# First-pair loads, the mask row table and an early second chunk in the opening of a block-sparse attention and gated FFN kernel

## The chip, the cores and the metric

The kernel runs on one core of a Trainium2 chip. The metric is device time in microseconds (us): 293.34 as the median of four runs. All times below are those of one profiled execution unless another source is named; its clock starts at the first instruction of the program.

## The reference

```python
scores = (q @ k.transpose(0, 1, 3, 2)) / np.sqrt(64)     # q, k, v: 4 x 8 heads x 768 x 64
mask = (abs(blk_i - blk_j) <= 1) | first_or_last_block    # blocks of 32 rows
mask[qb rows, sampled_blocks[qb] columns] = True          # three sampled blocks for each
scores = where(mask, scores, -1e9)
attn = softmax(scores)
x = heads_merged(attn @ v)                                # 3072 tokens x 512
out = (sigmoid(x @ w_gate) * (x @ w_val)) @ w_out         # 512 -> 1536 -> 512
```

Attention with a block mask for 4 batches of 8 heads, then a gated feed-forward network (FFN) over the 3072 tokens.

## The kernel before

**Tiling.** The 8 heads are taken as 4 pairs `p`; the 768 rows of a batch as 3 chunks of 256 queries. A chunk of a batch is numbered `n` (0 to 11). `attend(n, p, seq)` at L614 is the unit: three score steps (`tt`, each one two-bank PSUM tile of 128 keys x 2 x 512), three exponentials on ScalarE (ACT, L646), the product with V (L669), the reciprocal and scaling on VectorE (DVE, L677 and L680), and a turn of the result into `xT` (on TensorE, PE, for `n` below 3, L705). Units go in order of `n`, and within `n` of `p`. For `n` = 0 the mask is added in PSUM by extra matmuls of `e24` with `bias` (L628); for the other chunks the exponential is multiplied on DVE by a 0/1 `mask` (L654), which `build_mask` makes from the same two tables (L590 on PE, L598 on DVE). FFN work for a chunk (`ffn`, L719: gates at L731, output at L775) needs the results of all four pairs of that chunk.

**The table of mask rows.** `sbi` (the sampled blocks) and `mi` (a fixed mask) come in by small loads; four DVE operations (L548 to L554) make `mb16`; `expand` (L561) multiplies it on PE by the table `e24` and writes `bias` on DVE. `e24` is a constant that comes in two halves, one on SP's queue and one on ACT's (L354). `ident16` (L347) is what PE transposes with.

**The first inputs.** K and Q of pair 0 are split into an `early` part (2 of 6 column groups) and a `later` part (4 of 6). Early Q comes as 32-bit data on SP (`q_in`) and is cast on ACT; early K comes on POOL (`k_a`), whose loads cast to 16 bits on the way; later K comes on SP as 32-bit data (`k_in`, L476) and is cast on ACT (`k_b`, L484). Everything else of batch 0 comes on POOL as cast loads in the order of `FIRST` (L429), and behind them, on the same queue, the FFN weights (L511, L520). `turn_pe` (L435) transposes K and Q on PE and copies the result on DVE or ACT.

**What sets the order.** A planner (`Plan.run`) simulates the engines with a duration for each operation and a priority (lower goes first), and writes out one fixed program for each engine; nothing is reordered on the chip but by waiting. `LAND` gives the planner fixed landing times for the first loads; other loads land at a modelled time. Where PE has nothing ready in the plan before 22 us, the planner puts in short matmuls of a zero tile (`spin_op`, L370), which only keep PE busy. From the 19th unit on a chain (`CHAIN`) fixes PE's order by hand.

Of the kernel before, what the change touches and what calls it, by code (L numbers as in the profile page):

```python
# [10 lines left out]
f32 = mybir.dt.float32  # L11
# [4 lines left out]
B, H, S, D = 4, 8, 768, 64  # L16
BLK = 32
NB = S // BLK
NJ = S // 128
NP = H // 2  # L20
NCH = 3
# [6 lines left out]
VW = 66  # L28
SPIN = 22.0
NMASK = 1  # L30
FETCH = ((6, 1), (1, 2))
CHAIN, GLAG, OLAG, ROUND = 18, 5, 9, "SoVgggoo"
EDGES = [0, 768, 1536]
LAND = dict(sbi=2.9, mi=2.4, ident=3.1, e0=3.6, e1=3.9, q=2.9, kb=3.8, k=3.6)
FIRST = [
    ("k", 1), ("q", 1), ("k", 2), ("q", 2), ("v", 0), ("q", 0), ("k", 3), ("q", 3), ("v", 1), ("v", 2), ("v", 3),
]
HALF = [(0, 0), (0, 1), (0, 2), (0, 3)]
TURN_PE = 3
# [31 lines left out]
class Plan:  # L71
# [36 lines left out]
    def run(self):  # L108
# [10 lines left out]
        dma_free, mode, order, now = 0.0, None, [], 0.0  # L119
# [48 lines left out]
        while left:  # L168
            wake = []
            for e in LAT:  # L170
                if free[e] > now:
                    wake.append(free[e])
                    continue
                best = None
                for o in todo[e]:
                    t = 0.0
                    for d in o.deps:
                        if d.seen is None:
                            t = None
                            break  # L180
                        t = max(t, d.seen if d.eng != e or d.dma else d.end)
                    if t is None or any(d.end is None for d in o.behind):
                        continue
                    if t > now:
                        wake.append(t)
                        continue
                    t, where = places(o.allocs, e)
                    if t is None:
                        continue
                    if t > now:  # L190
                        wake.append(t)
                        continue
                    if o.mode == "row" and mode == "full" and o.paired:
                        s, _ = places([o.allocs[0], o.twin], e)
                        if s is None or s > now:
                            if s is not None:
                                wake.append(s)
                            if best is None:
                                best = o, where
                            continue  # L200
                    best = o, where
                    break
                if best is None and e == "PE" and now < self.spin_until and self.spin.writers[0].seen is not None:
# [12 lines left out]
                o, where = best  # L216
                take(o, where)
                o.eng = e
                dur, o.fn = o.ways[e]
                if e == "PE":  # L220
                    if o.mode != mode:
                        dur += 0.095
                    mode = o.mode
                o.start, o.end = now, now + dur
                if o.lands is not None:
                    o.seen = o.lands
                elif o.dma:
                    first = now + (3.2 if e == "POOL" else 1.9)
                    if o.dma > 0.15:
                        first = dma_free = max(dma_free, first) + o.dma  # L230
                    o.seen = first + 0.3 + o.slack
                else:
                    o.seen = o.end + LAT[e]
                free[e] = o.end
                for w in o.ways:
                    todo[w].remove(o)
                order.append(o)
                left -= 1
                wake.append(o.end)
# [21 lines left out]
def kernel(  # L261
# [11 lines left out]
    nc = tc.nc  # L273
# [9 lines left out]
    id_h = nc.inline_tensor(np.eye(128, dtype=np.float16), name="bb_ident")  # L283
# [11 lines left out]
    P = Plan()  # L295
# [33 lines left out]
    def one(shape, dt, name):  # L329
        b = Buf(None, None)  # L330
        b.tile = sing.tile(shape, dt, name=name)
        return b


    ident16 = one([128, 128], f16, "ident16")
    sbi = one([NB, 3], mybir.dt.int64, "sbi")
# [7 lines left out]
        lands=LAND["sbi"],  # L344
    )
    P.op(
        "ACT", 0.4, lambda: nc.scalar.dma_start(ident16(), id_h.ap()), writes=[ident16], prio=-98, dma=0.1,  # L347
        lands=LAND["ident"],
    )
    P.op("SP", 0.3, lambda: nc.sync.dma_start(mi(), mi_h.ap()), writes=[mi], prio=-99, dma=0.1, lands=LAND["mi"])  # L350
# [69 lines left out]
    def load_half(nm, b, p, prio, dur=0.72):  # L420
        cut = (nm, b, p) == ("q", 0, 0)
        js = later if cut else every
        if cut:
            c = one([128, 2, NJ - 2, 64], f16, "q16_late")
        else:
            c = sb(f"{nm}16" if nm != "v" else "vh", [128, 2, NJ, 64], f16)
        half16[nm, b, p] = stage[nm, b, p] = c
        o = P.op(
            "POOL", dur, lambda: nc.gpsimd.dma_start(c(), src[nm][b][:, 2 * p : 2 * p + 2, js]),  # L429
            writes=[c], prio=prio, dma=0.8 if cut else 1.0,  # L430
        )
        o.slack = 0.3 + b
        return o

    def turn_pe(nm, b, p, js, prio, behind=(), c=None, j0=0):  # L435
# [22 lines left out]
    def turn_dma(nm, b, p, prio):  # L458
# [6 lines left out]
            reads=[c], writes=[t], prio=prio, dma=1.3,  # L465
        )

    k_in, q_in = one([128, 2, NJ - 2, 64], f32, "k_in"), one([128, 2, 2, 64], f32, "q_in")
    k_a, k_b = one([128, 2, 2, 64], f16, "k16_a"), one([128, 2, NJ - 2, 64], f16, "k16_b")
    q_a = one([128, 2, 2, 64], f16, "q16_a")  # L470
    P.op(
# [1 line left out]
        lands=LAND["q"],  # L473
    )
    P.op(
        "SP", 0.5, lambda: nc.sync.dma_start(k_in(), src["k"][0][:, 0:2, later]), writes=[k_in], prio=-94, dma=1.0,  # L476
        lands=LAND["kb"],
    )
    P.op(
        "POOL", 0.82, lambda: nc.gpsimd.dma_start(k_a(), src["k"][0][:, 0:2, early]), writes=[k_a], prio=-95,  # L480
        dma=0.5, lands=LAND["k"],
    )
    P.op("ACT", 0.35, lambda: nc.scalar.copy(q_a(), q_in()), reads=[q_in], writes=[q_a], prio=-88)
    P.op("ACT", 0.56, lambda: nc.scalar.copy(k_b(), k_in()), reads=[k_in], writes=[k_b], prio=-67)  # L484
    for i, (nm, p) in enumerate(FIRST):
        last_in = load_half(nm, 0, p, -60 + i)
    late = None
# [18 lines left out]
    n = 0  # L506
# [292 lines left out]
                )  # L799

    seq, turned, late_loads = 0, [], []
    for n in range(B * NCH):
        b, c = divmod(n, NCH)
        if n == 1:
            for p in range(NP):
                turn_pe("q", 0, p, later, 9.0, [valued[0, 1]], j0=2 if p == 0 else 0)
            expand(2, 4, 2, scored[1:2])
            build_mask(1, 11.5, scored[4:5])
            build_mask(2, 14.5, [valued[0, 2]])
            build_mask(0, 26, [valued[0, 3]])  # L810
        for p in range(NP):
            attend(n, p, seq)
            seq += 3
        if b + 1 < B:
            for p in range(NP) if c == 0 else ():
                if (b + 1, p) in HALF:
                    for nm in "kq":
                        turn_pe(nm, b + 1, p, every, 3 * NP * (3 * b + 2))
                    cast_v(b + 1, p, 3 * NP * (3 * b + 2))
                    continue  # L820
# [67 lines left out]
```

## Time and profile before

| What | Value |
|---|---|
| four runs, us | 295.59, 292.96, 292.96, 293.71; median 293.34 |
| the profiled execution, its own time | 295.59 us |
| its span, first to last instruction | 292.3 us |
| busy share of PE, ACT, DVE, POOL | 98%, 71%, 67%, 5% |
| landing of `q_in`, `ident16`, `k_a`, `k_in` (issue plus time to landing) | 3.9, 3.7, 4.3, 5.2 us |
| landing of the cast loads of pairs 1 and 2, K, Q, K, Q | 6.7, 7.7, 8.8, 9.8 us |
| landing of V of pair 0, later Q of pair 0 | 10.7, 11.4 us |
| landing of the first gate weight, the first value weight | 20.4, 24.6 us |
| first exponential; last of chunk 0; first FFN matmul | 8.52; 22.88; 26.02 us |

The program's own time is 3.3 us above its span. A busy PE is not a PE doing useful work: the spins count as busy, and matmul ends are modelled. The landing times are worked out from the issue time of each load and its time from issue to landing. DMA engines are busy almost throughout the first 44 us.

### The profile page before, as it was taken

How to read it: one execution, taken by the hardware profiler on the slowest of the kernel's cores; microseconds unless marked ns; L12 is line 12 of the kernel's file. 1: busy time of each engine (PE TensorE's matmuls, PEld its weight loads, DVE VectorE, ACT ScalarE, POOL GpSimd, SP SyncE). 2: the span in 40 equal slices, each digit the busy share in tenths (PEclk: the TensorE clock that was granted, in tenths of full speed). 3: DMA queues.
4: the chain of work that ended last, by engine and by line, in shares of the span. 5: the costliest groups of instructions: out<-in, count | busy, mean ns of one | idle time of the engine just before them, and what ended most of it. 6: DMA issues, size and time to landing. Idle time of an engine off the chain costs nothing.

```text
span 292.3 us, 8127 instructions
## 1 busy us (share of the span) xinstructions
PE 287.3 (98%) x3417; PEld 212.4 (73%) x3417; DVE 195.9 (67%) x458; ACT 206.7 (71%) x321; POOL 14.1 (5%) x23
## 2 busy tenths in 40 slices
PE   7999999999999999999999999999999999999995
PEld 6677776786677867767767777777777776777764
DVE  3359968997897667756876876765765765773330
ACT  3685589897888678678768768767777777773331
POOL 8820000000000000000000000000000000000000
PEclk9999999999999999999999999999999999999999
DMA  7999995993899664014566564010010120121003
GB/s 142 196 211 209 206 296 163 265 249 25 252 233 207 92 211 94 20 47 147 134 209 184 146 214 95 16 56 29 27 56 15 41 57 9 48 56 33 14 36 109
DMA packets 50788, 35.43 MB, mean 121 GB/s; under 512 B 31376, under 2 KB 47808, under 8 KB 50752
## 3 DMA queue, kind: packets, MB, share of 16 engines
q1 hardware_dynamic: 43576, 27.97, 35.9%
q0 software_dynamic: 6960, 6.88, 14.3%
q8 instruction: 26, 0.43, 0.6%
q10 hardware_dynamic: 216, 0.07, 0.1%
q14 instruction: 10, 0.08, 0.1%
HBM read 28.42 MB, written 6.29 MB: 119 GB/s over the span
## 4 chain that ended last, share of the span: by engine, by line
PE 97%; DMA 2%; ACT 0%; issue 0%
PE psum L731 44%; PE psum L775 23%; PE psum L628 14%; PE psum L669 13%; PE psum L447 1%; DMA e<-bb_e 1%; PE psum L590 1%; PE psum L705 1%; PE psum L370 1%; DMA sbi<-in_sampled_blocks_dram 1%; PE psum L566 0%; ACT y L792 0%
## 5 line engine op out<-in xcount | busy, mean ns | idle before, releaser
L646 ACT ACTIVATE pt<-psum 128x1024 f16<-128x1024 f32 x144 | 139.1, 1026 | 25.6 <-PE psum L628 25.5
L654 DVE TENSOR_TENSOR pt<-pt,mask 128x1024 f16<-128x1024 f16 x132 | 89.4, 688 | 46.0 <-ACT pt L646 45.9
L731 PE MATMUL psum<-x,wv 128*128 128x256 f16 x576 | 86.5, 273 | 0.0
L731 PE MATMUL psum<-x,wg 128*128 128x256 f16 x576 | 86.4, 272 | 0.0
L750 ACT ACTIVATE tg<-psum 128x256 f32<-128x256 f32 x144 | 56.0, 390 | 41.6 <-PE psum L731 41.1
L775 PE MATMUL psum<-wo,h 128*128 128x512 f16 (+1 forms) x300 | 75.4, 372 | 0.0
L757 DVE SCALAR_TENSOR_TENSOR h<-tg,psum 128x256 f16<-128x256 f32 x144 | 58.2, 417 | 24.1 <-ACT tg L750 23.6
L731 PEld LDWEIGHTS <-wv 128*128 128x128 f16 x576 | 55.5, 98 | 8.0 <-issue 1.7
L731 PEld LDWEIGHTS <-wg 128*128 128x128 f16 x576 | 53.4, 98 | 7.8 <-issue 1.3
L669 PEld LDWEIGHTS <-pt 128*128 128x128 f16 x1152 | 42.4, 98 | 9.6 <-issue 0.8
L628 PE MATMUL psum<-qT,kT 64*128 64x256 f16 x576 | 45.8, 274 | 0.0
L669 PE MATMUL psum<-v,pt 128*128 128x65 f16 x1152 | 44.3, 193 | 0.0
L775 PEld LDWEIGHTS <-h 128*128 128x128 f16 x300 | 26.1, 98 | 22.8 <-issue 7.6
L628 PEld LDWEIGHTS <-kT 64*128 64x128 f16 x576 | 24.6, 95 | 19.6 <-issue 16.7
L680 DVE TENSOR_TENSOR x<-psum,rz 128x256 f16<-128x256 f32 x48 | 20.4, 424 | 1.6
L792 ACT ACTIVATE y<-psum 128x512 f32<-128x512 f32 (+1 forms) x22 | 12.7, 578 | 12.3 <-PE psum L775 12.3
L677 DVE RECIPROCAL rz<-psum 128x4 f32<-128x4 f32 x48 | 8.6, 180 | 5.7 <-PE psum L669 5.6
L370 PE MATMUL psum<-zero 128*64 128x128 f16 x47 | 6.2, 296 | 1.0 <-DVE zero L340 1.0
L628 PE MATMUL psum<-bias,e 64*128 64x256 f16 x48 | 6.8, 305 | 0.0
L370 PEld LDWEIGHTS <-zero 128*64 128x64 f16 x47 | 5.0, 161 | 1.6 <-DVE zero L340 1.0
L598 DVE TENSOR_SCALAR mask<-psum 128x512 f16<-128x512 f32 x9 | 6.1, 683 | 0.0
L415 DVE CAST k<-ks 128x768 f16<-128x768 f32 x10 | 5.5, 553 | 0.0
(53 smaller groups left out, 71.9 us busy)
## 6 DMA issues: line engine op xcount, KB each, us to landing
out_dram<-y SPq DMA_DIRECT2D x23, 256.0 KB, 2.6
ks<-in_k_dram SPq DMA_DIRECT2D x12, 384.0 KB, 3.3
qs<-in_q_dram SPq DMA_DIRECT2D x12, 384.0 KB, 4.0
vs<-in_v_dram SPq DMA_DIRECT2D x12, 384.0 KB, 4.6
wg<-in_moe_w_gate_dram POOLq DMA_DIRECT2D x2, 768.0 KB, 13.5
wv<-in_moe_w_val_dram POOLq DMA_DIRECT2D x2, 768.0 KB, 16.5
wo<-in_moe_w_out_dram POOLq DMA_DIRECT2D x3, 512.0 KB, 22.5
vh<-in_v_dram POOLq DMA_DIRECT2D x4, 192.0 KB, 7.0
```

What stands on the lines that cost most here:

```text
L370: "PE", dur, lambda: nc.tensor.matmul(t()[0:64], zero()[:, 0:64], zero(), start=True, stop=True),
L628: nc.tensor.matmul(st()[:, hd, jj * CH : (jj + 1) * CH], l[r, 2 * tt + jj, :], m[r, 2 * c : 2 * c + 2, :], start=not (own and masked), sto ...
L646: lambda st=st, pt=pt: nc.scalar.activation(pt().rearrange("p h j q -> p h (j q)"), st(), AF.Exp, scale=SCALE),
L654: nc.vector.tensor_tensor(t, t, mask()[:, c, tt].unsqueeze(1).to_broadcast([128, 2, 512]), op=ALU.mult)
L669: nc.tensor.matmul(o()[:, 2 * jq + hd, 0:65], pts[j // 2]()[:, hd, j % 2, jq * 128 : jq * 128 + 128], v_[:, hd, j, 0:65], start=(j == 0), ...
L677: P.op("DVE", 0.2, lambda: nc.vector.reciprocal(rz(), o()[:, :, 64:65]), reads=[o], writes=[rz], prio=seq - 5)
L680: lambda: nc.vector.tensor_tensor(x16().rearrange("p j (h d) -> p (j h) d", d=64), o()[:, :, 0:64], rz().to_broadcast([128, 4, 64]), op=AL ...
L731: nc.tensor.matmul(t()[:, z : z + w], wt()[:, i, f * 128 : (f + 1) * 128], xT[g, i]()[:, 0:w], start=(i == 0), stop=(i == NP - 1),)
L750: lambda tg=tg, a=pair[0]: nc.scalar.activation(tg()[:, 0:w], a[0]()[:, a[1] : a[1] + w], AF.Tanh, scale=0.5),
L757: lambda tg=tg, a=pair[1], h_=h_: nc.vector.scalar_tensor_tensor(h_()[:, 0:w], tg()[:, 0:w], 1.0, a[0]()[:, a[1] : a[1] + w], op0=ALU.add, ...
L775: nc.tensor.matmul(py()[:, m], hts[g, f]()[:, tt * 128 : (tt + 1) * 128], wo()[:, f, m], start=(f == 0), stop=(f == NF - 1),)
L792: lambda py=py, y=y, m=m: nc.scalar.activation(y()[:, m], py()[:, m], AF.Copy, scale=0.5),
```

## The change

- Later K of pair 0 moves from SP (32-bit, cast on ACT) to POOL as a cast load, straight into `k_b`, second on that queue. `k_in`, its load on SP and the cast on ACT go.
- SP's half of `e24` thereby follows `q_in` directly. The priority of `ident16` falls behind that of ACT's half of `e24`.
- `FIRST` now starts with later Q of pair 0, then K and Q of pair 1, V of pair 0, and then pairs 2 and 3.
- The units are taken in the order (n, p) = (0,0), (1,0), (0,1), (0,2), (0,3), (1,1), ... The turn of later Q of pair 0, the second `expand` and the mask of chunk 1 are planned for that; the later Q of the other pairs keeps its place.
- The planner's landing times and its model of POOL's loads are changed. A branch that never ran is left out.

```diff
+AHEAD, Q0P, M1P = 1, -39.2, 14
-LAND = dict(sbi=2.9, mi=2.4, ident=3.1, e0=3.6, e1=3.9, q=2.9, kb=3.8, k=3.6)
+LAND = dict(sbi=1.7, mi=1.6, ident=3.2, e0=3.4, e1=3.3, q=3.1, kb=4.4, k=3.5)
 FIRST = [
-    ("k", 1), ("q", 1), ("k", 2), ("q", 2), ("v", 0), ("q", 0), ("k", 3), ("q", 3), ("v", 1), ("v", 2), ("v", 3),
+    ("q", 0), ("k", 1), ("q", 1), ("v", 0), ("k", 2), ("q", 2), ("k", 3), ("q", 3), ("v", 1), ("v", 2), ("v", 3),
 ]
...
                 if o.lands is not None:
                     o.seen = o.lands
+                    dma_free = max(dma_free, o.lands - 0.3) if e == "POOL" else dma_free
                 elif o.dma:
-                    first = now + (3.2 if e == "POOL" else 1.9)
+                    first = now + (2.5 if e == "POOL" else 1.9)
...
-        "ACT", 0.4, lambda: nc.scalar.dma_start(ident16(), id_h.ap()), writes=[ident16], prio=-98, dma=0.1,
+        "ACT", 0.4, lambda: nc.scalar.dma_start(ident16(), id_h.ap()), writes=[ident16], prio=-92, dma=0.1,
...
-        o.slack = 0.3 + b
+        o.slack = b
...
-    P.op(
-        "SP", 0.5, lambda: nc.sync.dma_start(k_in(), src["k"][0][:, 0:2, later]), writes=[k_in], prio=-94, dma=1.0,
-        lands=LAND["kb"],
-    )
...
+    P.op(
+        "POOL", 0.72, lambda: nc.gpsimd.dma_start(k_b(), src["k"][0][:, 0:2, later]), writes=[k_b], prio=-94,
+        dma=0.8, lands=LAND["kb"],
+    )
...
-    P.op("ACT", 0.56, lambda: nc.scalar.copy(k_b(), k_in()), reads=[k_in], writes=[k_b], prio=-67)
...
-    for n in range(B * NCH):
+    order = [(n, p) for n in range(B * NCH) for p in range(NP)]
+    order.insert(AHEAD, order.pop(NP))
+    for n, p in order:
         b, c = divmod(n, NCH)
-        if n == 1:
-            for p in range(NP):
-                turn_pe("q", 0, p, later, 9.0, [valued[0, 1]], j0=2 if p == 0 else 0)
+        if (n, p) == (1, 0):
+            turn_pe("q", 0, 0, later, Q0P, scored[:1], j0=2)
             expand(2, 4, 2, scored[1:2])
-            build_mask(1, 11.5, scored[4:5])
+            build_mask(1, M1P, scored[2:3])
+        if (n, p) == (1, 1):
+            for i in range(1, NP):
+                turn_pe("q", 0, i, later, 9.0, [valued[0, 1]])
             build_mask(2, 14.5, [valued[0, 2]])
             build_mask(0, 26, [valued[0, 3]])
-        for p in range(NP):
-            attend(n, p, seq)
-            seq += 3
+        attend(n, p, seq)
+        seq += 3
```

More of the change, by code (lines that the diff above doesn't have):

```diff
@@ L466, in turn_dma @@
         )
-    k_in, q_in = one([128, 2, NJ - 2, 64], f32, "k_in"), one([128, 2, 2, 64], f32, "q_in")
+    q_in = one([128, 2, 2, 64], f32, "q_in")
     k_a, k_b = one([128, 2, 2, 64], f16, "k16_a"), one([128, 2, NJ - 2, 64], f16, "k16_b")
@@ L801 @@
     seq, turned, late_loads = 0, [], []
[L802 removed]
+    order = [(n, p) for n in range(B * NCH) for p in range(NP)]
+    order.insert(AHEAD, order.pop(NP))
+    for n, p in order:
         b, c = divmod(n, NCH)
[L804 to L806 removed]
+        if (n, p) == (1, 0):
+            turn_pe("q", 0, 0, later, Q0P, scored[:1], j0=2)
             expand(2, 4, 2, scored[1:2])
[L808 removed]
+            build_mask(1, M1P, scored[2:3])
+        if (n, p) == (1, 1):
+            for i in range(1, NP):
+                turn_pe("q", 0, i, later, 9.0, [valued[0, 1]])
             build_mask(2, 14.5, [valued[0, 2]])
             build_mask(0, 26, [valued[0, 3]])
[L811 to L820 removed]
+        attend(n, p, seq)
+        seq += 3
+        if p == NP - 1 and b + 1 < B and c == 0:
+            for p in range(NP):
                 for nm in "kqv":
```

## The prediction

> **What bounds the kernel now.** I read the chain of waits first, on the whole span and then on its first 40 us.
>
> ```profile
> PE 97%; DMA 2%; ACT 0%; issue 0%
> ...
> 2.30 3.51 DMA e<-bb_e
> 5.81 0.14 issue
> 5.94 0.43 PE psum L566 x2
> ...
> 8.72 0.97 PE psum L628 x8
> ...
> 18.02 0.54 PE psum L628 x8
> ```
>
> PE is the chain for 97% of the span, and the 2% of DMA is all at the start: the mask row table cannot be expanded until the half of `e24` that SP issues at 2.30 has landed at 5.81, and PE stands idle for it. The last two lines show the same eight score matmuls at 0.97 us and at 0.54. PE's timeline says when that changes, and ACT's what follows from it.
>
> ```profile
> 11.02 0.42 PE L628 MATMUL psum<-qT,kT 64*128 64x256 f16 x2
> ...
> 12.77 0.27 PE L628 MATMUL psum<-qT,kT 64*128 64x256 f16 x2
> ```
>
> ```profile
> 8.52 1.02 ACT L646 ACTIVATE pt<-psum 128x1024 f16<-128x1024 f32 x1 [2.67 <-PE psum L628]
> 9.73 1.02 ACT L646 ACTIVATE pt<-psum 128x1024 f16<-128x1024 f32 x1 [0.19 <-PE psum L628]
> 11.48 1.02 ACT L646 ACTIVATE pt<-psum 128x1024 f16<-128x1024 f32 x1 [0.72 <-PE psum L628]
> 13.30 2.85 ACT L646 ACTIVATE pt<-psum 128x1024 f16<-128x1024 f32 x3 [0.80 <-PE psum L628]
> ```
>
> Until 12.0 us PE works at half speed (the granted clock of the stretches reads 1.00 throughout, so the matmuls are the evidence), and ACT waits for PE before nearly every exponential. So the only time to be won is what PE loses in the opening. For the profiled execution: nothing on the chain until 5.94, less eight early transposes worth 0.26 (twelve take 0.39 later), 5.7; spins after that, the L370 pieces of the chain, 0.18 + 0.10 + 0.10 + 0.32 + 0.24 + 0.10 + 0.44 + 0.17 = 1.65; and half of the slow work, (12.0 − 5.94 − 0.94 of spins)/2 = 2.6. Together 9.9 us. After 18.02 the chain has no spin and no wait of note, so what is won before then is kept if PE is still fed.
>
> **The change, part by part.** The sum is made on the profiled execution's own 295.59 us (span 292.3), which is 2.25 above the median; I carry the difference over to the median.
>
> *The start.* With `k_in` gone, SP's half of `e24` is issued at 1.80, in `k_in`'s place, instead of 2.30, and stands behind 128 KB, not 128 + 256. Its latency is bounded by the rows of these queues (KB of each, and the us from issue to landing; `ident16`, 32 KB on ACT, took 2.3).
>
> ```profile
> k_in<-in_k_dram SPq DMA_DIRECT2D x1, 256.0 KB, 3.4
> q_in<-in_q_dram SPq DMA_DIRECT2D x1, 128.0 KB, 2.7
> ...
> k_a<-in_k_dram POOLq DMA_DIRECT2D x1, 64.0 KB, 3.1
> ```
>
> Landing 1.80 + 2.3 = 4.1 at best; at worst 5.3, the same 3.51 after the earlier issue. I take 4.5, by `q_in`'s 2.7, the load just ahead in that queue. With the 0.14 of issue PE's first link moves from 5.94 to 4.6: **−1.3 us** (−0.6 to −1.7). The new order puts the wait for `e24` ahead of the eight transposes of `k_a` and `q_a` on PE. `k_a` is there at 4.3 and `q_a` at 4.28, so below a landing of 4.3 this wait costs nothing, and beyond it all PE work queues behind it, as it does now behind the first scores.
>
> *The clock.* PE opened at 12.0, 6.1 us after it last stood idle. If it again needs 6.1 us of work, it opens at 10.7 and the slow loss stays 2.6: **0**. If the opening stays at 12.0, the 1.3 us are won at half speed, +0.7. At best it needs no more than the 3.1 us of spins from 0.99 to 4.08, which did not open it, so not before 7.7: slow loss 1.5, −1.1. I take 0, since the 6.1 us is the only stretch that did open it.
>
> The Trainium skill ("TensorE: Matmul & The Clock Gate", Part 1) says the clock opens after a full busy window of about 3.4 us of a free-running counter. By that page alone it would be an estimate of 8.0 to 11.4, some 0.5 us better than I take; the trace shows only the one opening, after 6.1.
>
> *Later K on POOL.* The 0.62 cast on ACT goes, on an engine that then idles 2.67: nothing. `k_b` is issued at 2.04, in place of the first K load. It lands between 5.1 (`k_a`'s 3.1) and 6.7 (what that K load reached with half as much again). Cast loads that follow one another land 0.95 us apart for 384 KB read, so 256 KB behind `k_a`'s 4.3 give 4.95, and I take 5.1. PE reaches its transposes at 4.6 + 0.43 + 0.6 = 5.6: covered by 0.5; at the far end PE waits 1.1 and the gain falls by as much. Nothing taken.
>
> The skill ("DMA: Bandwidth & Descriptors", Specifications) speaks against this move: a POOL load has a first byte after about 1 us, one from SP after about 0.6. By it `k_b` would be 0.4 later, an estimate of 5.5, still under the 5.6; the rows agree in kind, 3.1 for 64 KB on POOL against 2.7 for 128 KB on SP.
>
> *The queue behind it.* K and Q of pair 1 are issued two places, 1.43 us, later, but only later Q's 256 KB are new ahead of them: landing 7.4 and 8.3 instead of 6.7 and 7.7, needed not before some 9.5 (9.62 now). K and Q of pair 2 come 1.6 later, at 10.4 and 11.4; K's transposes ran at 12.02. Bytes ahead of the weights are the same, so 20.4 and 24.6 stay. ACT's issue order stays too: the planner has ACT free at 0.65, but the clearing of `e24` seen only at 0.48 + 0.20 = 0.68, so `ident16` goes first whatever its new priority.
>
> *The early unit (1,0).* It adds no instruction. On PE, by the pieces of the chain: eight transposes (of 32 at 1.08) 0.27, 12 scores 0.76, 24 products 0.87, turn 0.22, six mask matmuls 0.65, 2.8 us in all that now run after 20 us. They can take the place of the spins at 12.22, 13.93 and 17.85, 0.71, and at best of those at 7.19 and 8.48 too, 0.56. Against that, scores of pair 1 now stand behind the second table on DVE (0.68). Between −1.3 and +0.7 I take **−0.5**, since the scores of pair 0, which the spins between 6 and 9 fill up to, wait on copies as before. DVE gets three masks of 0.68 and three products of 0.69 early; it has room.
>
> ```profile
> 8.00:12.00 4.00, 4.00 (x41) 2.02 (x37) 0.72 (x2) 2.57 (x3) 3.63 (x6) 1.00 1.30 192
> 12.00:16.00 4.00, 4.00 (x83) 3.25 (x81) 1.37 (x5) 3.21 (x4) 2.73 (x4) 1.00 1.31 203
> ...
> 24.00:28.00 4.00, 4.00 (x42) 2.71 (x38) 3.96 (x10) 2.35 (x4) 0.00 (x0) 1.00 1.16 212
> ```
>
> DVE, the third busy figure, has 0.72 and 1.37 of 4 us where the masks go, and 3.96 where they come from. ACT takes three exponentials, 3.07 us, ahead of chunk 0's, and has gaps of 0.72, 0.80 and 0.74 to take them; so the last of chunk 0 moves from 22.88 to between 22.88 + 3.07 − 1.3 − 2.26 = 22.4 and 24.7, and the first FFN matmul, 3.1 behind it, to 25.5 to 27.8. What fills PE till then is the 2.8 us above.
>
> Sum: −1.3 + 0 − 0.5 = **−1.8 us**: 293.8 for the profiled execution, 291.5 on the median. With one term at its end at a time (start −0.6 to −1.7, spins −1.3 to +0.7) its own range is 290.7 to 292.7.
>
> **Rivals.** *The clock opens early.* PE works unbroken from 4.6 and opens at 7.7: −1.3 − 1.1 − 0.5 = −2.9, 290.4; with the best ends −1.7 − 1.1 − 1.3 = −4.1, 289.2. For it: the idle 0.97 before 5.94 goes. Against it: 3.1 us of spins did nothing.
>
> *No gain.* Either ACT's half of `e24`, still issued at 1.80, is the late one (the chain only shows that it is no later than 5.81), or the time won is lost before the value weight of 24.6. Then only spins are won, 0 to −0.7: 292.6 to 293.3.
>
> *Slower: ACT is handed (1,0) first and PE runs dry before the FFN.* If the gaps on ACT are not filled and the start wins nothing, chunk 0's exponentials end at 22.88 + 3.07 = 25.95. PE has 2.8 us to do meanwhile, so it decides from an end later than 22.88 + 2.8 = 25.7; the price is 0.3 (293.6) if those 2.8 all run in that time and 3.07 (296.4) if none does. For it: PE is planned in fixed order. Against it: ACT's gaps are waits for PE's scores, which (1,0), with 12 score matmuls where chunk 0 has 24, supplies sooner.
>
> **How the numbers follow.** Forecast 0.46, early clock 0.25, no gain 0.16, slower 0.13. A measurement here tells about 1%, 2.9 us, from no change: below 290.4 faster, above 296.3 slower. The early-clock case is put whole on the faster side: 0.25. Of the slower case a little under half is put beyond 1%, as its upper end is just there and nothing shown rules it out: 0.06. The rest, 0.69, is within 1%. The range, 289.6 to 294.4, cuts 0.07 off the early-clock end and about 0.1 off the slower one.
>
> **What would show it.** The wait for `e24` ends near 4.5 and the first table matmul starts near 4.6; the first exponential starts near 7.2 instead of 8.52; the 128x256 score matmuls drop from 0.42 to 0.27 near 10.7; three exponentials more are done by 23.9; no spin after 13; the first FFN matmul lies within 25 to 27; from there the chain is PE alone, shifted. It is wrong if the first table matmul is still near 5.9, if PE spins or waits between 14 and 27, or if the half-speed stretch ends at 12 or later.

## The result, and the profile after

| | before | changed |
|---|---|---|
| median, us (runs) | 293.32 (79) | 293.88 (53) |
| ratio, 95% interval | | 1.0021 [1.0012, 1.0031] |
| profiled execution, own time (span), us | 295.59 (292.3); again 292.80 (291.0) | 292.95 (291.1); again 292.95 (291.2) |

The change costs 0.6 us. The predicted range holds that, and so does "within 1%", but the forecast was a gain of 1.8 us, and none of it came. PE starts each execution at half speed, and the trace records when its clock opens to full speed (a pair of first scores took 0.40 in the first profile of before, ahead of the opening, and 0.28 in the second, behind it). The profile of before that the prediction rests on is of an execution that opened late, at 12.3 us; a second one opened at 4.5. It is the second that is compared with the changed kernel, which opened at 4.2 and 4.0.

The chain of waits, first on the whole span of the changed kernel (the page's shares by engine), then in its first 40 us (start, length, what):

```profile
PE 93%; DMA 3%; POOL 2%; ACT 0%; issue 0%; ACTq 0%; POOLq 0%
```

```profile
2.05 0.71 POOL k_b L482
2.76 0.71 POOL q_late L431
...
7.03 7.75 DMA k<-in_k_dram
14.83 0.53 PE psum L449 x12
...
26.48 1.03 ACT pt L647
```

The same view of before, second execution:

```profile
4.18 5.77 DMA q<-in_q_dram
...
11.25 13.83 DMA wv<-in_moe_w_val_dram
25.13 1.48 PE psum L731 x12
```

The table of mask rows has left the chain, as predicted. In its place stands POOL's queue: eight loads issued one behind the other, and behind them the K of pair 3, which lands at 14.8. In the second execution of before, the same queue bound the opening by the first value weight: FFN work had begun and then waited for it until 25.13. In the changed kernel FFN work isn't ready for it: the weight lands at 26.4, the first FFN matmul comes at 28.08.

PE's timeline of the changed kernel (start, length, what, in brackets the idle time before and its releaser):

```profile
4.58 0.30 PE L567 MATMUL psum<-e,mb 128*64 128x256 f16 x2 [0.61 <-DMA e<-bb_e]
...
6.11 0.41 PE L449 MATMUL psum<-ident,k_b 128*64 128x128 f16 x8 [0.75 <-DMA k_b<-in_k_dram]
...
6.57 0.28 PE L629 MATMUL psum<-bias,e 64*128 64x256 f16 x2
...
10.02 0.30 PE L449 MATMUL psum<-ident,q 128*64 128x128 f16 x4 [0.57 <-DMA q<-in_q_dram]
...
14.83 0.53 PE L449 MATMUL psum<-ident,k 128*64 128x128 f16 x12 [0.76 <-DMA k<-in_k_dram]
```

and of before, second execution:

```profile
5.94 0.30 PE L566 MATMUL psum<-e,mb 128*64 128x256 f16 x2 [0.86 <-DMA e<-bb_e]
...
6.25 0.41 PE L447 MATMUL psum<-ident,k_b 128*64 128x128 f16 x6
...
6.76 0.28 PE L628 MATMUL psum<-bias,e 64*128 64x256 f16 x2
...
14.04 0.53 PE L447 MATMUL psum<-ident,k 128*64 128x128 f16 x12 [0.98 <-DMA k<-in_k_dram]
```

The table's matmul moved from 5.94 to 4.58 and the first scores only from 6.76 to 6.57: between them PE's order has the transposes of later K, and `k_b` is there at 6.07. ACT's first exponentials say the same, changed kernel and then before:

```profile
7.22 2.85 ACT L647 ACTIVATE pt<-psum 128x1024 f16<-128x1024 f32 x3 [1.81 <-PE psum L629]
```

```profile
7.41 2.85 ACT L646 ACTIVATE pt<-psum 128x1024 f16<-128x1024 f32 x3 [1.53 <-PE psum L628]
```

Where the time goes after that is seen best in a ledger of PE. I charge each matmul that isn't a spin with the usual interval to the next one of its shape (the mean between 100 and 250 us); what is left of a stretch is lost to waits, spins, half speed and changes from one kind of matmul to another. The useful work is 266.6 us in all kernels, so 266.6 plus the sum of a row is the start of the last matmul, to 0.3 us; most of these 0.3 are the ledger's zero, POOL's first instruction, which stands at 0.24 in the views. The last column is in the time of the views. One profile, of the first run with units back, had a mean granted clock of 0.872 and isn't read.

| lost by PE, us, in | 0–6 | 6–10 | 10–24 | 24–28 | 28–40 | 40–60 | 60–100 | later | sum | clock opens |
|---|---|---|---|---|---|---|---|---|---|---|
| before | 5.62 | 2.58 | 3.81 | 1.24 | 1.65 | 1.49 | 2.40 | 3.45 | 22.2 | 12.3 |
| before, again | 5.45 | 0.87 | 4.85 | 1.11 | 1.20 | 1.49 | 2.40 | 3.44 | 20.8 | 4.5 |
| changed | 5.37 | 1.41 | 4.33 | 1.84 | 1.28 | 1.64 | 1.61 | 3.44 | 20.9 | 4.2 |
| changed, again | 5.35 | 1.57 | 3.95 | 1.68 | 1.37 | 1.96 | 1.61 | 3.44 | 20.9 | 4.0 |
| units back, again | 5.35 | 1.86 | 5.39 | 2.07 | 1.81 | 1.17 | 2.90 | 3.46 | 24.0 | 5.4 |
| only later K on POOL | 5.30 | 2.41 | 3.77 | 1.13 | 1.56 | 1.75 | 2.17 | 3.45 | 21.5 | 10.1 |
| same, planned at 5.2 | 5.01 | 1.29 | 4.68 | 0.67 | 1.38 | 1.45 | 1.89 | 3.50 | 19.9 | 4.8 |
| same, again | 5.15 | 1.90 | 4.27 | 1.62 | 1.43 | 1.21 | 2.62 | 3.45 | 21.6 | 5.3 |
| that with the new FIRST | 4.89 | 2.87 | 5.11 | 2.10 | 1.71 | 1.21 | 2.65 | 3.45 | 24.0 | 4.2 |
| changed, planned at 5.2 | 5.53 | 2.37 | 3.85 | 1.85 | 3.79 | 1.17 | 2.22 | 3.47 | 24.3 | 10.0 |
| planner's model alone | 5.75 | 1.95 | 3.69 | 0.91 | 1.24 | 2.06 | 2.40 | 3.45 | 21.4 | 9.2 |

Nothing differs after 100 us, in any kernel of the table. Of the changed kernel against before, again: 0.1 won up to 6 us, 0.5 to 0.7 lost up to 10, 0.5 to 0.9 won up to 24, 0.6 to 0.7 lost up to 28, 0.2 to 0.6 lost from there to 60, and 0.8 won from 60 to 100. The profiles are 0.15 us apart in their own time, the medians 0.56.

### The profile page after: what moved, and what is told of

Read it like the earlier page. It is cut to its first block, busy times and chain, and to the rows that moved or that the text cites. A ratio compares the mean times of both kernels' runs of the same rounds, so it can differ in the third digit from the quotient of the medians.

```text
span 291.1 us, 8117 instructions
## 1 busy us (share of the span) xinstructions
PE 284.3 (98%) x3412; PEld 210.6 (72%) x3412; DVE 194.6 (67%) x456; ACT 206.3 (71%) x322; POOL 14.8 (5%) x24
## 4 chain that ended last, share of the span: by engine, by line
PE 93%; DMA 3%; POOL 2%; ACT 0%; issue 0%; ACTq 0%; POOLq 0%
PE psum L732 44%; PE psum L776 23%; PE psum L629 13%; PE psum L670 12%; DMA k<-in_k_dram 3%; PE psum L591 1%; PE psum L449 1%; PE psum L706 1%; POOL k L431 0%; POOL q L431 0%; ACT pt L647 0%; POOL k_a L478 0%; POOL vh L431 0%; POOL k_b L482 0%; POOL q_late L431 0%
## 5 line engine op out<-in xcount | busy, mean ns | idle before, releaser
L776 PE MATMUL psum<-wo,h 128*128 128x512 f16 (+1 forms) x300 | 74.5, 372 | 0.0
L629 PE MATMUL psum<-qT,kT 64*128 64x256 f16 x576 | 45.1, 271 | 0.1
L776 PEld LDWEIGHTS <-h 128*128 128x128 f16 x300 | 26.3, 98 | 23.4 <-issue 7.0
L793 ACT ACTIVATE y<-psum 128x512 f32<-128x512 f32 (+1 forms) x23 | 13.3, 579 | 12.3 <-PE psum L776 12.3
L681 DVE TENSOR_TENSOR x<-psum,rz 128x256 f16<-128x256 f32 x48 | 20.4, 424 | 1.6
L408 DVE CAST v<-vs 128x768 f16<-128x768 f32 x10 | 5.6, 555 | 1.8 <-DMA vs<-in_v_dram 1.8
L629 PE MATMUL psum<-bias,e 64*128 64x256 f16 x48 | 6.0, 273 | 0.0
L372 PE MATMUL psum<-zero 128*64 128x128 f16 x42 | 5.0, 280 | 1.0 <-DVE zero L342 1.0
```

The source lines that it names most:

```text
L629: nc.tensor.matmul(st()[:, hd, jj * CH : (jj + 1) * CH], l[r, 2 * tt + jj, :], m[r, 2 * c : 2 * c + 2, :], start=not (own and masked), sto ...
L681: lambda: nc.vector.tensor_tensor(x16().rearrange("p j (h d) -> p (j h) d", d=64), o()[:, :, 0:64], rz().to_broadcast([128, 4, 64]), op=AL ...
L776: nc.tensor.matmul(py()[:, m], hts[g, f]()[:, tt * 128 : (tt + 1) * 128], wo()[:, f, m], start=(f == 0), stop=(f == NF - 1),)
L793: lambda py=py, y=y, m=m: nc.scalar.activation(y()[:, m], py()[:, m], AF.Copy, scale=0.5),
```

## The experiments

All ratios are to runs of the kernel before that were measured alongside, with their 95% intervals. Every edit makes the planner write a new order, so each ratio is that of the edit and of its plan together. Two runs settle what compares with what: each kernel once more, unedited.

> The kernel before, unchanged, as a control and for a second trace. Expected 293.3 with an interval that holds 1.000. Loads theory: the first K load of pair 1 lands near 6.7 and the first value weight near 24.6 in this trace too; if those landings scatter by a microsecond from run to run, the late landings of the changed kernel say nothing. Clock theory: PE opens to full speed at another moment than 12.0, and the span moves by half of the difference.

> The changed kernel, unchanged, for a second trace. Expected 293.9. Loads theory: the K load of pair 1 lands near 8.7, K of pair 3 near 14.8, the first value weight near 26.4 again, and PE waits for them again, whatever the clock does. Chance theory: the landings go back to 7.4, 12.9 and 24.6.

Before again: 1.0006 [0.9983, 1.0028]; the changed kernel again: 1.0019 [1.0001, 1.0037]. So half-speed work up to 12 us, of which the prediction's sum of 9.9 us took 2.6, belongs to one execution and not to the kernel. By the ledger the late opening cost 22.2 − 20.8 = 1.4 us. The landings scatter too: K of pair 1 came at 6.71 and 6.69 in the two profiles of before, but K of pair 3 at 12.4 and 14.0 and the first gate weight at 20.5 and 21.4.

An open clock can close again, and the mean granted clock of each execution tells where it did: one closing of 3.41 us takes 0.006 off the mean. It closed in 9 of 12 executions of "the order alone" below, in 8 of 12 of "the table first", in 3 of 6 of "later K planned at 5.2 in the changed kernel", and in one or two of those of "later K on SP", "that with the new FIRST" and "first weights cut smaller". The profiles of all six show a closing. Where it seldom closed, the executions without a closing were about as slow, so it isn't the cause of their loss.

### Parts of the change

**Units back.** The changed kernel, units in their natural order.

```diff
-AHEAD, Q0P, M1P = 1, -39.2, 14
+Q0P, M1P = 9.0, 11.5
...
-    order.insert(AHEAD, order.pop(NP))
...
-            turn_pe("q", 0, 0, later, Q0P, scored[:1], j0=2)
+            turn_pe("q", 0, 0, later, Q0P, [valued[0, 1]], j0=2)
...
-            build_mask(1, M1P, scored[2:3])
+            build_mask(1, M1P, scored[4:5])
```

> The changed kernel with its loads as they are, but the units in the old order: (1,0) after (0,3), later Q of pair 0 turned where it was. Loads theory (the opening is now set by POOL's queue, on which later K and later Q stand ahead of pair 1): the cast loads still land late (first K of pair 1 near 8.7 us, K of pair 3 near 14.8, first value weight near 26.4) and PE has less to do between them, so 294 to 295 us. Unit theory (the early unit holds back chunk 0 and the FFN): the first FFN matmul goes back to 26 us or earlier and the time falls to 292 to 292.8.

> The changed kernel with units in their natural order once more, for its profile, which was that of a disturbed execution the first time. Ledger of PE's time (time not spent on useful matmuls at their steady rate) by stage, against the changed kernel: if the early unit wins in the opening and pays in the first FFN stretch, this one loses about 0.5 us more between 10 and 24 us, and 0.5 to 0.7 us less between 24 and 28. If the load order alone holds the FFN back, it loses at least as much as the changed kernel (1.7 to 1.8 us) between 24 and 28 too, first FFN matmul later than 26. Ratio 1.005 to 1.009 in both.

1.0070 [1.0042, 1.0099], and again 1.0069 [1.0042, 1.0096]. The ledger loses 1.1 us more than the changed kernel between 10 and 24 us, 0.2 more between 24 and 28, and 1.3 more between 60 and 100. So the early unit, with the plan that comes with it, is worth about 1.4 us of the median (0.5% of 293), not all of it in the opening, and it isn't what holds the FFN back: without it the first FFN matmul comes at 28.49, with it at 28.08. PE's timeline without it shows what does:

```profile
9.45 0.53 PE L449 MATMUL psum<-ident,k 128*64 128x128 f16 x12 [0.81 <-DMA k<-in_k_dram]
...
15.80 0.53 PE L449 MATMUL psum<-ident,k 128*64 128x128 f16 x12 [1.17 <-DMA k<-in_k_dram]
...
28.49 0.61 PE L732 MATMUL psum<-x,wg 128*128 128x256 f16 x4
```

**Later K on 32-bit, on SP.** The changed kernel, but later K behind the table on SP, and cast on ACT.

```diff
-LAND = dict(sbi=1.7, ... kb=4.4, k=3.5)
+LAND = dict(sbi=1.7, ... kb=4.8, k=3.5)
...
-        "POOL", 0.72, lambda: nc.gpsimd.dma_start(k_b(), ...), prio=-94,
+        "SP", 0.5, lambda: nc.sync.dma_start(k_in(), ...), prio=-92, dma=1.0,
...
+    P.op("ACT", 0.56, lambda: nc.scalar.copy(k_b(), k_in()), ...)
```

> The changed kernel with later K again as a 32-bit load on SP, now behind SP's half of the table, and cast on ACT; the rest as changed. Loads theory: POOL's queue is shorter by 256 KB read, so every load of pair 1 and behind lands 0.6 to 1 us earlier than in the changed kernel, the weights too, and the time falls to 292.5 to 293.2. Unit theory: as the changed kernel, 293.6 to 294.2.

1.0073 [1.0043, 1.0103]. `k_in` landed at 8.06 and later Q at 8.28; PE stood idle for 2.16 us before 8.32. So the table can't simply go first on SP, as the next run shows too: later K has to leave that queue. (This profile took 298.14 us, with the clock closed for 6.83; the other six executions, without, took 295.6 to 296.3.)

**The table first, nothing else.** The kernel before with `k_in` behind SP's half of the table.

```diff
-        ... writes=[k_in], prio=-94, dma=1.0,
+        ... writes=[k_in], prio=-92, dma=1.0,
```

> The kernel before with one edit: SP's half of the table is issued ahead of later K. Loads theory: the table lands near 4.6 instead of 5.8, later K near 5.4 instead of 5.2, nothing else moves, so 0.5 to 1.2 us faster than before (292.1 to 292.8). If the opening is set by when the clock opens and not by the table: 293.3, as before.

1.0063 [1.0040, 1.0085]. The table's matmul ran at 4.64, but `k_in` landed at 7.26 instead of 5.21. PE's timeline, and the stretches (busy us of PE, its weight loads, DVE, ACT, POOL, then the granted clock, the DMA share and GB/s):

```profile
7.96 0.64 PE L447 MATMUL psum<-ident,k_b 128*64 128x128 f16 x8 [2.71 <-ACT k_b L484]
```

```profile
6.00:8.00 2.00, 0.04 (x2) 0.05 (x4) 0.00 (x0) 0.62 (x1) 2.00 (x4) 0.97 1.25 194
8.00:10.00 2.00, 2.00 (x20) 1.24 (x20) 0.42 (x1) 0.08 (x1) 1.57 (x3) 0.50 1.31 201
```

PE stands idle for 2.7 us and the clock then falls to half until 11.3. The four executions without a closing took 295.5 to 296.1, no less than the rest. An early table that makes PE wait for later K is worse than a late one.

**The order alone.** New FIRST and units; later K, the table and `LAND` as before. The planner's new model of POOL's loads and the priority of `ident16` stay as in the changed kernel.

```diff
+AHEAD, Q0P, M1P = 1, -39.2, 14
...
-    ("k", 1), ("q", 1), ("k", 2), ("q", 2), ("v", 0), ("q", 0), ...
+    ("q", 0), ("k", 1), ("q", 1), ("v", 0), ("k", 2), ("q", 2), ...
...
```

> The kernel before with the new order of the cast loads and the new order of units alone; later K on SP ahead of the table, as before. Loads theory: POOL's landings lie near those of before plus later Q's 0.7, time 293.0 to 293.6. Unit theory: the FFN starts 1 to 2 us later, time 294 to 295.

1.0063 [1.0036, 1.0090], first FFN matmul at 31.34. The clock was closed from 30.6 to 34.0; the three executions without a closing took 293.4 to 295.1 (middle one 294.4), the nine with one 295.5 in the median, so here the closings may be half of the loss.

**Later K on POOL, table first, alone.** FIRST and units as before; `LAND`, the planner's new model of POOL's loads and the priority of `ident16` as in the changed kernel.

```diff
-LAND = dict(sbi=2.9, ... kb=3.8, k=3.6)
+LAND = dict(sbi=1.7, ... kb=4.4, k=3.5)
...
-        "SP", 0.5, lambda: nc.sync.dma_start(k_in(), ...), prio=-94, dma=1.0,
+        "POOL", 0.72, lambda: nc.gpsimd.dma_start(k_b(), ...), prio=-94, dma=0.8,
```

> Later K as a cast load on POOL and the table ahead, alone: the order of the other cast loads and the order of units as before (the planner's new landing times stay). Loads theory: 256 KB more on POOL's queue puts every load behind 1 to 1.5 us later than before, PE waits for pair 1 and has no early unit to fill the wait: 294 to 295.5. Unit theory: 292 to 293.

1.0008 [0.9990, 1.0026]: the table's 1.3 us alone is worth nothing that shows. `k_b` lands at 5.87, and in the kernel before later K was ready at 5.27 + 0.62 = 5.89, the end of its cast; its transposes stand ahead of the first scores.

**The same, with later K planned at 5.2**, so that PE's order has the first scores ahead of those transposes.

```diff
-LAND = dict(sbi=1.7, ... kb=4.4, k=3.5)
+LAND = dict(sbi=1.7, ... kb=5.2, k=3.5)
```

> Later K on POOL and the table ahead, alone, as in the earlier run, with the planner told that later K lands at 5.2 on its clock (measured: 5.85 on the trace's, which is 0.68 ahead) instead of 4.4. If PE's order, which puts the transposes of later K ahead of the first scores, gives back what the table won: the first scores start near 5.6 instead of 6.6 and the time falls by 0.4 to 0.8 us, 292.8 to 293.1. Stream theory: the first exponential comes earlier and the time stays, 293.3 to 293.7.

> Later K on POOL, table first, later K planned at 5.2, loads and units otherwise in the order of before, once more: a ratio of 0.996 to 0.9995 if its 0.22% is the kernel's; 0.9995 to 1.002 if it was the draw of that call's clock openings (its profile opened at 4.6 us).

0.9978 [0.9962, 0.9994], and again 0.9985 [0.9962, 1.0007]. It is the only version below before in both of its comparisons, by about 0.2%, and the second interval reaches 1. PE's timeline:

```profile
4.55 0.42 PE L567 MATMUL psum<-e,mb 128*64 128x256 f16 x2 [0.58 <-DMA e<-bb_e]
...
5.60 0.28 PE L629 MATMUL psum<-bias,e 64*128 64x256 f16 x2
...
6.14 0.41 PE L449 MATMUL psum<-ident,k_b 128*64 128x128 f16 x8
```

Here the early table does bring the scores forward, by 1.16 us (6.76 to 5.60), and the first exponential from 7.41 to 6.25; in the second profile they start at 5.83 and 6.48. Of that the median keeps about a half: the FFN still waits for the value weight, which lands at 25.0 and, in the second profile, at 26.3.

**That with the new FIRST**, units natural.

```diff
-    ("k", 1), ("q", 1), ("k", 2), ("q", 2), ("v", 0), ("q", 0), ...
+    ("q", 0), ("k", 1), ("q", 1), ("v", 0), ("k", 2), ("q", 2), ...
```

> Later K on POOL and planned late (the version that was 0.2% faster than before), plus only the new FIRST; units in their natural order. If later Q ahead of everything else is what costs: ratio 1.003 to 1.006, that is 0.5 to 0.7% above that version, PE waiting for K and Q of pair 1 that land near 8.7 and 10.0 instead of 7.0 and 8.0. If the +0.7% of the changed kernel with natural units came of the transposes of later K ahead of the first scores: ratio 0.998 to 1.001.

1.0105 [1.0079, 1.0131], 1.2 to 1.3% above the version it is built on: the costliest part of the change. First exponential at 6.16, K of pair 1 at 9.42, first FFN matmul at 28.10. In this profile (295.79 us) the clock fell to half from 11.0 to 14.5, but four executions in which it didn't took 295.1 to 296.3 as well. So the load order, with its plan, loses what the table wins, and more.

**The early unit one place later**, behind (0,1), and later Q behind pair 1 in FIRST.

```diff
-AHEAD, Q0P, M1P = 1, -39.2, 14
+AHEAD, Q0P, M1P = 2, -37.3, 14
...
-    ("q", 0), ("k", 1), ("q", 1), ("v", 0), ...
+    ("k", 1), ("q", 1), ("q", 0), ("v", 0), ...
```

> The changed kernel with the early unit one place later, (0,0), (0,1), (1,0), and later Q of pair 0 loaded behind K and Q of pair 1, its turn planned there. Stream theory: pair 1 lands 0.7 us earlier than in the changed kernel, the weights land as late as there (25.8 to 26.4), so 293.3 to 294.0, at best level with before. Unit theory (it only matters that (1,0) fills PE's waits): 292.3 to 293.

1.0025 [1.0003, 1.0046]: K and Q of pair 1 land at 7.04 and 8.12 and V at 9.8, before its 10.7 to 11.0 in the kernel before. But K and Q of pair 2 land at 10.9 and 12.2 instead of 8.7 and 9.7 to 10.0, and the first FFN matmul comes at 29.47.

### Loads and weights

**A load that nobody reads.** The kernel before with an unread cast load of 256 KB, second on POOL.

```diff
+    P.op("POOL", 0.72, lambda: nc.gpsimd.dma_start(spare(), src["k"][1][:, 0:2, later]), writes=[spare], ...)
```

> The kernel before plus one cast load that nothing reads, 256 KB read, second on POOL's queue, where the change puts later K (and the planner knows of it). Stream theory (POOL's queue of inputs and weights is what the opening waits for): every load behind it lands 0.7 to 1.0 us later, first value weight near 25.8 to 26, and the time grows by 0.5 to 1.0 us, 293.8 to 294.4. If PE or the clock sets the opening: the landings move and the time stays, 293.2 to 293.5.

0.9991 [0.9970, 1.0013]. K of pair 1 landed at 7.98 instead of 6.7, the value weight at 26.1, the first FFN matmul came at 27.39 (with the clock open only from 12.4), and the time is the same. So a bare delay of POOL's queue by one place isn't what costs.

**First weights cut smaller.**

```diff
-EDGES = [0, 768, 1536]
+EDGES = [0, 512, 1536]
```

> The kernel before with the gate and value weights cut at column 512 instead of 768, so that the first two weight loads are a third smaller: the first value weight lands near 22.5 instead of 24.6 to 25.1. Stream theory with the first FFN matmul waiting for it: 0.3 to 0.8 us faster, 292.5 to 293. If the FFN starts late for another reason (the units of pair 3): no change, 293.3.

1.0146 [1.0113, 1.0178]. The value weight lands at 22.3 and the FFN starts at 25.95, so the weights aren't all that holds it; the loss comes after 28 us (3.02 and 2.32 between 28 and 60).

### The planner

**Loads planned late**: the changed kernel with `kb=5.3` and all other POOL loads 0.9 later in the plan.

```diff
-        o.slack = b
+        o.slack = 0.9 + b
```

> The changed kernel with the planner told the landing times that were measured (later K 0.9 later, every other cast load of batch 0 0.9 later); what runs is the same, only PE's order can change. If the loads themselves bound the opening: 293.5 to 294.2, as the changed kernel. If PE's fixed order, planned for earlier loads, is what makes it wait: 0.5 to 1.5 us faster, 292.4 to 293.4.

1.0100 [1.0062, 1.0138]: told of later landings, the planner makes a kernel that is 0.8% slower, not faster. First exponential 6.79; between 40 and 60 us PE loses 3.43 us, 1.37 of them waiting for `h` from DVE (0.34 before 44.75, 1.03 before 47.57).

**The planner's model alone**: the kernel before, loads and units unedited.

```diff
+                    dma_free = max(dma_free, o.lands - 0.3) if e == "POOL" else dma_free
...
-                    first = now + (3.2 if e == "POOL" else 1.9)
+                    first = now + (2.5 if e == "POOL" else 1.9)
...
-        o.slack = 0.3 + b
+        o.slack = b
```

> The kernel before with only the planner's three changed constants of POOL's loads (first byte 2.5 instead of 3.2, slack smaller by 0.3, the queue free after fixed landings); loads, LAND, FIRST and the order of units as before. If the loss of the changed kernel comes from what is loaded and scored in another order: no difference, ratio 0.999 to 1.001, weights at 21.4 and 25.0, first FFN matmul near 25. If it comes from the fixed order that the planner makes from more hopeful landings: slower by 0.1 to 0.5%, ratio 1.001 to 1.005, with PE waiting for K, Q or V of pairs 1 to 3 in the opening.

1.0022 [1.0001, 1.0043]: as much as the whole change, with no load or unit moved. The first exponential is at 9.46 (the clock opened at 9.2), the first FFN matmul at 24.71.

**Later K planned late in the kernel before.**

```diff
-LAND = dict(... kb=3.8, k=3.6)
+LAND = dict(... kb=4.6, k=3.6)
```

> The kernel before with only the planner's landing of later K at 4.6 instead of 3.8: PE has the first scores ahead of the transposes of later K; every load as before. The table and the cast later K are there within 0.1 us of each other (5.81, 5.85), so if the gain of the same edit with later K on POOL came from the earlier table, it is worth at most 0.4 us here (transposes out of the way of the first scores): ratio 0.998 to 1.000 with the first exponential 0.3 to 0.5 earlier. If it came from the order that the planner then makes of all the rest: ratio 0.997 to 0.999, although the table is late.

1.0063 [1.0045, 1.0081]; it neither gained what it would by the table nor what it would by the plan. The table's matmul ran at 6.37, the first exponential at 8.73 and the first FFN matmul at 26.35; the clock opened at 10.2 here, so these compare with 8.52 and 26.02 of the first execution of before. Why it is 0.6% slower isn't shown.

**Later K planned at 5.2 in the changed kernel.**

```diff
-LAND = dict(sbi=1.7, ... kb=4.4, k=3.5)
+LAND = dict(sbi=1.7, ... kb=5.2, k=3.5)
```

> The changed kernel, with the planner's landing of later K at 5.2 instead of 4.4, so that PE has the first scores ahead of its transposes. If the swallowed start is what the change lacks: first exponential near 6.3 instead of 7.2 and ratio 0.998 to 1.000 (as the same edit took the kernel with later K on POOL from 1.0008 to 0.9978). If the rest (pairs 1 to 3 and weights 1 to 2 us later, chunk 0 held back by the early unit) sets the time: first exponential as early, and the ratio stays at 1.001 to 1.003, with PE waiting for K and Q of pairs 1 to 3 by about 1 us more than before.

1.0096 [1.0068, 1.0124]. My theory that the swallowed start is what the changed kernel lacks falls here: the edit made it 0.7% slower. Its first exponential came at 7.36, as the clock opened only at 10.0, so the gain at the start wasn't to be seen in this profile; but the loss is elsewhere, 3.79 us between 28 and 40, where PE's timeline has

```profile
28.53 0.39 PE L629 MATMUL psum<-qT,kT 64*128 64x256 f16 x4 [0.84 <-ACT pt L647]
...
30.09 0.71 PE L629 MATMUL psum<-qT,kT 64*128 64x256 f16 x8 [0.63 <-ACT pt L647]
```

and the clock is at half speed from 30.5 to 33.9. Of its six executions the three with a closing took 296.1 to 297.1, the three without 294.4 to 295.4.

## Why the prediction was right or wrong

**The start.** "PE's first link moves from 5.94 to 4.6" was right (4.58); **−1.3 us** was wrong. The step that failed is later K "covered by 0.5. Nothing taken". I took a landing of 5.1 from bounds of 5.1 and 6.7; it was 6.07 (6.05 in the second profile). And I had PE reach these transposes at 5.6, by half-speed durations; at full speed it was done with the table and the early transposes at 4.9 and stood before later K until 6.11. So a wait of 1.2 us was put at nothing, and of the 1.3 the first scores keep 6.76 − 6.57 = 0.2. In the kernel before, table and later K were late together, at 5.81 and 5.89. Bringing one of two equally late inputs forward gains nothing unless PE's order can go on without the other: the table's part alone gave 1.0008, and 0.9978 and 0.9985 once the first scores were planned ahead of later K, though a new plan alone moves the time by as much (see the planner's runs above).

**The queue behind it.** "Only later Q's 256 KB are new ahead of them: landing 7.4 and 8.3" failed, and so, it seems, did "20.4 and 24.6 stay". In these two kernels the landings go by place in POOL's queue: the fourth, fifth and sixth load of POOL land at 8.7, 10.0 and 11.0 in before again (K and Q of pair 2, V) and at 8.6, 10.0 and 11.0 in the changed kernel (K and Q of pair 1, V). So two places cost K and Q of pair 1 two whole loads, 8.63 − 6.69 = 1.9 and 9.98 − 7.67 = 2.3 us (2.1 and 2.5 in the second profile), not 0.7, and PE waits 0.57 for that Q. Each of the two new loads has its share: with later Q alone ahead (the order alone) this K and Q land at 7.9 and 8.9, with later K alone (later K on POOL) at 6.8 and 8.9. It is no law of the queue: over all profiles the fourth load landed between 8.1 and 9.4. The first weights come at 22.8 and 26.4, in the second profile at 22.0 and 25.8, against 20.5 and 24.6, then 21.4 and 25.1, in before. That is later, but two profiles of another single kernel, the one planned at 5.2, lie 1.3 apart (21.4 and 22.7; 25.0 and 26.3). The issues of the changed kernel (KB written, us from issue to landing):

```profile
k_b<-in_k_dram POOLq DMA_DIRECT2D x1, 128.0 KB, 4.0
q_late<-in_q_dram POOLq DMA_DIRECT2D x1, 128.0 KB, 4.0
k_a<-in_k_dram POOLq DMA_DIRECT2D x1, 64.0 KB, 3.1
```

That a 256 KB load takes a place of its own isn't all of it: the DMA engines moved less while it lasted. Part of that is counting, as the trace has the bytes that are written: later K counts 256 KB as the 32-bit `k_in` and 128 KB as the cast `k_b`, which is up to 128 KB in 6 us, 22 of the GB/s. The stretch of 4 to 10 us (last number GB/s), before again, only later K on POOL, changed:

```profile
4.00:10.00 6.00, 4.86 (x88) 3.41 (x89) 2.24 (x6) 3.52 (x5) 5.94 (x9) 1.00 1.20 199
```

```profile
4.00:10.00 6.00, 5.42 (x58) 3.73 (x60) 1.38 (x4) 2.64 (x4) 5.94 (x9) 1.00 1.20 167
```

```profile
4.00:10.00 6.00, 4.11 (x72) 2.78 (x72) 2.03 (x5) 3.46 (x5) 5.88 (x9) 1.00 1.14 144
```

The six profiles with later K and later Q as second and third on POOL moved 144 to 150, those with one of them there 152 to 186, those with neither 179 to 203 (before 199 and 203).

**The early unit.** **−0.5** was about right in its place, though not through the spins alone, of which the chain still holds a group at 17.10: between 10 and 24 us the changed kernel loses 0.5 to 0.9 less than before, and 1.1 to 1.4 less than without the unit. But the gain is given back at once: the first FFN matmul came at 28.08, beyond "25.5 to 27.8", and 24 to 28 loses 0.6 to 0.7 more than before. The rival that I had for this, ACT handed (1,0) first, isn't it: the exponentials of chunk 0 were done by 24.25, short of its 25.7. DVE's timeline shows the last steps:

```profile
24.03 0.18 DVE L678 RECIPROCAL rz<-psum 128x4 f32<-128x4 f32 x1 [1.30 <-PE psum L670]
...
25.88 0.17 DVE L678 RECIPROCAL rz<-psum 128x4 f32<-128x4 f32 x1
...
27.43 0.28 DVE L711 COPY x<-psum 128x256 f16<-128x256 f16 x1
```

Four units' results go through DVE in a row from 24.03 to 27.7, as the products come late and together. What goes with that is the load order: the kernels with later Q first in FIRST start the FFN at 27.7 to 33.5, the one with it behind pair 1 at 29.47, those with FIRST as before at 24.3 to 27.4. Load order and plan changed together in all of them.

**The clock.** "**0**" isn't contradicted, but was no property of the kernel. That PE was at half speed until 12 was one execution's; "9.9 us" to be won was too much. The rival of an early clock doesn't tell the two kernels apart in the profiles compared: it opened early in both. How often each kernel opens late isn't on record, so it stays possible that the medians differ by that too. In mechanism the rival "no gain" came nearest, with its "time won is lost before the value weight", though what ate the time was later K and the queue, not the weight. In number the measured 293.9 lies in the range of the slower rival, 293.6 to 296.4, but not for its reason. Two readings in the prediction are a little off and decide nothing: a table that lands at 5.3 leaves a gain of 0.5, not 0.6, and POOL's cast loads landed 1.0 us apart, not 0.95.

**What I had not counted.** Of the 0.8 us won between 60 and 100, most is fewer changes of kind, that is, of PE going from matmuls of one shape to those of another: PE goes over to scores 12 times there in before and 9 times in the changed kernel. Each visit costs about 0.19 (0.095 going, 0.093 coming back). PE's timeline of before, again:

```profile
64.29 0.60 PE L731 MATMUL psum<-x,wv 128*128 128x256 f16 x4
64.73 0.60 PE L731 MATMUL psum<-x,wg 128*128 128x256 f16 x4
65.26 0.61 PE L628 MATMUL psum<-qT,kT 64*128 64x256 f16 x8
65.81 0.61 PE L731 MATMUL psum<-x,wv 128*128 128x256 f16 x4
```

Four gate matmuls take 0.44 when more of them follow and 0.53 when scores do. No one wrote this into the change: it comes out of the plan made anew.

**The sum, in medians.** From before: later K on POOL with the table first, +0.1% (its interval holds zero); the new FIRST on top, +0.7% in all; the early unit takes it back to +0.2%. Planned at 5.2 the first step is −0.2%, but then the new FIRST makes it +1.05%. The steps don't add, since each new plan costs or wins some tenths of a per cent itself: +0.2% for three constants, +0.6% for one. The whole effect of the change, +0.2%, is no larger than that: it says that the gain of 1.8 us wasn't there, not which step left the rest.

**Open.** Why the DMA engines moved less with both partial loads on POOL, beyond the counting: their packets can be seen to take longer, not why. Why a bare delay of the queue by one place (the unread load) costs nothing and the load order 0.6%: that the first keeps the order in which PE needs the loads is what I hold for likely, and no run shows it by itself. The 0.2% of the best version rests on two comparisons, and how much of it is the table and how much the plan wasn't told apart.

## What to carry to other kernels

Before an input is brought forward, look for the others that land within a few tenths of it: the gain is the time to the next one in the engine's order. On a queue that is always full, count the places that a load loses as well as the bytes, and ask who moves back. Where a planner writes the order out, a change of its constants alone is a control run that belongs beside the change: here it moved the time as much as the change did.

## What the runs showed of the hardware

The granted clock of one and the same kernel opened at 4.5 us in one execution and at 12.3 in another, with the same spins ahead of it. Over the 19 profiles that are read the openings fall in two groups, eleven at 4.0 to 5.9 us and eight at 9.2 to 12.4, with none between. Once open it closed again in six profiles, five times for 3.41 us and once for 6.83. The Trainium skill ("TensorE: Matmul & The Clock Gate", Part 1) gives a free-running window of 3413 ns, and these lengths agree with it to the hundredth. Its "±500ns" for the moment of opening is said of sustained matmul activity; no run here shows that, as the first spins end at about 4.1 us and PE then waits, and the spread is 8.4 us. The prediction held that spins of 3.1 us don't open the clock, from the one trace where they had not; in four others, which opened at 4.0 to 4.2, nothing but spins ran ahead.

Single packets of POOL's loads, which mostly take 0.06 to 0.08 us, took up to 1.0 us in the changed kernel. Their time above the usual one, summed over the 16 engines between 5 and 10 us, was 1.9 and 2.5 us in the two profiles of before and 11.6 and 9.2 in the two of the changed kernel.
